# Two first products of layer 1, and the first group's weights, inside the end of an attention

## The chip, the cores and the metric

The kernel runs on one core of a Trainium2 chip. The metric is device time in microseconds (us) of one execution. Before the change three runs took 815.57, 817.38 and 818.75 us; the median is 817.38 us. The traced execution took 815.6 us, of which its trace spans 813.8 us. Times below are counted from the start of that span.

## The reference, cut to what matters

Clustered attention is followed by two feed-forward layers. `x` is the attention's output with the heads side by side (1536 tokens, 512 wide).

```python
scores = np.where(mask, scale * q @ k.T, -1e9)      # B=2, H=8, S=768, D=64; mask: same nearest centroid
attn = softmax(scores); x = attn @ v
h = x @ w_in;   g = np.maximum(0.01 * h, h);  x1 = g @ w_out          # layer 1: 512 -> 2048 -> 512
h = x1 @ w_in2; g = P(h) / (Q(h) + 1e-6);     out = g @ w_out2        # layer 2: P cubic, Q quadratic
```

The weights arrive as 64-bit floats, so each piece of them is rebuilt as a 32-bit number on the core before it is used.

## The kernel before, in words

Every product is made of three matmuls on split numbers (high part times high part, high times low, low times high), so each tensor comes as a pair: `ph`/`pl` for the attention's weights, `xh`/`xl` for `x`, `wih`/`wil` and `woh`/`wol` for the layers' weights, `gh`/`gl` for `g`.

**Attention** works on 96 units of 128 queries (one head, 768 keys). `run` (L674) is a software pipeline written out by hand: iteration i issues, in this order, the row maximum of unit i (DVE), the division of earlier units' `e` (POOL, for the last unit DVE), the transposes `pT` of unit i-4 in two halves, each followed by its cast `ph` on ACT, the `o` matmuls of a group whose last unit this is, exp (ACT), the scores of unit i+1, more `o` matmuls, and `pl = pT - ph` on DVE. The `pT` halves go round three PSUM buffers, so a half waits for the `pl` of the half three before it. Three units make a group; its twelve last `o` matmuls are issued in iterations i+1 to i+3 of its last unit. Then `merge_copy` (ACT, `tmp`), `merge_add` (DVE, `xf`) and, seven iterations later, `finish` (POOL, two or four instructions that write `xh` and `xl`). Each engine runs its instructions in the order in which they are issued here, and what waits holds up all that stands behind it on its engine.

**A piece of weights** (128 x 512) is loaded by SP's queue into a stage (`st`), and rebuilt by ACT (Abs, L787, into `wf`), DVE (a shift, L794, and two merges, L800), ACT (cast to the high part, L807) and POOL (the low part, L810). `Weights.step` issues one such operation of the two oldest pieces in turn. `wsta` is a stage of two buffers, opened in the attention at iteration 84; `wstb`, of two more, lies on memory that the attention has used.

**The layers** run over nine groups of hidden columns. Group 0 of layer 1 has 2 x 128 hidden columns, in a `wi` of two pieces (rebuilt early and kept in a scratch, so only cast and low part are left) and a `wo` of two pieces. A step is (group, token block of 512, 128 hidden columns): twelve `h` matmuls, leaky (ACT, `h<-h`), `gh` (ACT), `gl` (DVE), and three steps later (LAG = 3) twelve `y` matmuls (`back`). Each iteration ends with its share of the next group's rebuilding. `h` has four PSUM buffers, the four `y` have one each; after a block's last step DVE copies them out (`acc`).

In the kernel before, group 0's `wi` is finished in the attention, its `wo` only in part: the pool for it is opened when the attention's memory is free.

Of the kernel before, what the change touches and what calls it, by code (L numbers as in the profile page):

```python
# [17 lines left out]
P = 128  # L18
# [11 lines left out]
def clustered_attention_moe_moe2(  # L30
# [69 lines left out]
    x1 = {}  # L100
# [34 lines left out]
        return a * 2 + u  # L135

    class Attention:
        def __init__(self, actx):
            def pool(nm, bufs, **kw):
                return actx.enter_context(tc.tile_pool(name=nm, bufs=bufs, **kw))  # L140
# [378 lines left out]

        def trans_p(self, u, part):  # L520
            un = self.unit[u]
            pp = self.ring("pT") if u == NU - 1 else self.ptile("pT")
            n = T // 2
            for kt in range(n):
                k0 = (part * n + kt) * P
                nc.tensor.transpose(pp[:, kt * P:(kt + 1) * P], un["e"][:, k0:k0 + P], ident)  # L526
            un["pT", part] = pp[:, 0:n * P].rearrange("p (t n) -> p t n", t=n)
# [146 lines left out]
        def run(self, extra, fill):  # L674
# [10 lines left out]
            for i in range(first, NU + TL + 11):  # L685
# [17 lines left out]
                if live:  # L703
                    self.trans_p(i - TL, 0)
                    self.hi(i - TL, 0)
                    self.trans_p(i - TL, 1)
                    self.hi(i - TL, 1)
                if ok and r == QT - 1:
# [29 lines left out]
                if i == last_prep:  # L738
                    self.pc.close()
                    extra[0]()  # L740
                elif i > last_prep:
                    extra[1](i >= NU + TL)

    class Weights:
        def __init__(self, pools):
# [8 lines left out]
        def add(self, key, src, which, par, wide, store=None):  # L754
# [5 lines left out]

            def alloc():
                pool = self.pools[which, par]
                for x in "hl":
                    t = pool.tile([P, 4, 512], F32R, tag=x, name=f"{which}{x}")
                    hold[x] = t[:, 0:rows // wr].rearrange("p a (b c) -> p (a b) c", c=cols)
# [127 lines left out]

    def queue_group(n):
        for which in ("wi", "wo"):
            if (n, which) in scratch:
                weights.add((which, n), scratch[n, which], which, n % 2, False)
            else:
                weights.add((which, n), weight_source(n, which), which, n % 2, WIDE)

    def queue_scratch(n, whiches=("wi", "wo")):
        for which in whiches:
# [7 lines left out]
    with tc.manual_schedule():  # L910
# [26 lines left out]
        def open_weights(which, par, **kw):  # L937
            wpools[which, par] = wctx.enter_context(
                tc.tile_pool(name=f"{which}{par}", bufs=1, **kw)
            )  # L940

        def open_early():
            while weights.work:
                weights.step()
            weights.wst.clear()
            open_weights("wi", 0, side="right")
            open_stage("wsta", side="right")
            queue_group(0)

        def early_step(late):  # L950
            if late or weights.waits_for(("wi", 0)):
                weights.step(1)

        weights = Weights(wpools)
        with ExitStack() as actx:
            att = Attention(actx)
            att.run((open_early, early_step), (open_start, weights))

        for nm in (("wo", 0), ("wi", 1), ("wo", 1)):
            open_weights(*nm)  # L960
        yp = wctx.enter_context(tc.tile_pool(name="yp", bufs=1))
        x1["c"] = [yp.tile([P, NCT, BLK], F32R, name=nm) for nm in ("xhc", "xlc")]
        accs = yp.tile([P, NCT * NT], F32, name="acc")
        gp_ = wctx.enter_context(tc.tile_pool(name="gp", bufs=3))
        ew = wctx.enter_context(tc.tile_pool(name="ew", bufs=2))
        open_stage("wstb")
        hps = wctx.enter_context(tc.tile_pool(name="hps", bufs=4, space=PSUM))
        yps = wctx.enter_context(tc.tile_pool(name="yps", bufs=1, space=PSUM))
        prep_consts()
        while weights.waits_for(("wi", 0)):  # L970
            weights.step()

        LNC = float(2.0 ** -LN_SHIFT)
        LAG = 3
        steps = [
# [22 lines left out]
        def wide(i):  # L998
            return width(groups[steps[i][0]][0])

        def make_h(i):
            n, j, f = steps[i]
            wih, wil = weights.get(("wi", n))
            w = wide(i)
            hp = hps.tile([P, 512], F32, tag="h", name="h")[:, 0:w]
# [14 lines left out]

        def hi(i):
            d = st[i]
            d["gh"] = gp_.tile([P, 512], F32R, tag="gh", name="gh")[:, 0:wide(i)]
            nc.scalar.copy(d["gh"], d["h"])  # L1024

        def lo(i):
            d = st[i]
            d["gl"] = gp_.tile([P, 512], F32R, tag="gl", name="gl")[:, 0:wide(i)]
            nc.vector.tensor_tensor(d["gl"], d["h"], f32(d["gh"]), op=ALU.subtract)  # L1029

        def leaky(i):
# [91 lines left out]
        def next_x():  # L1123
            j, o, a = later.pop(0)
            t0 = j * 512
            for nm, lo, hi in (("a", 0, 2 * BLK), ("b", 2 * BLK, 3 * BLK), ("c", 3 * BLK, NT)):
# [6 lines left out]
        later = []  # L1133
        for i in range(NS + LAG):
            if i < NS and steps[i][1:] == (0, 0):
                n1 = steps[i][0] + 1
# [2 lines left out]
                if n1 < len(groups):  # L1139
# [13 lines left out]
            if later:  # L1153
                next_x()
            if i >= LAG:
                collect(i - LAG)
# [4 lines left out]
            if i < LAG and weights.waits_for(("wo", 0)):  # L1161
                weights.step(4)
            if i == LAG - 2:
                while weights.waits_for(("wo", 0)):
                    weights.step()


_INS = ['q', 'k', 'v', 'centroids', 'moe_w_in', 'moe_w_out', 'moe2_w_in', 'moe2_w_out', 'moe2_a', 'moe2_b']
# [26 lines left out]
```

## Time and profile before

| what | value |
|---|---|
| median of three runs | 817.38 us |
| traced execution / its span | 815.6 us / 813.8 us |
| PE busy | 789.7 us, 97% of the span |
| DVE, ACT, POOL busy | 660.6, 526.9, 400.4 us |
| last attention unit's exp / first `h` matmul | 263.77 us / 273.99 us |
| first `y` matmul | 285.18 us |

The shares are means over an attention, in which PE, DVE and ACT are all near full, and two layers, in which PE alone is. What the change is worth is read from the stretch from 263 to 300 us, where one passes into the other: there each engine's timeline tells when it was free and what it waited for.

### The profile page before, as it was taken

Reading aid. Unit: us, or ns where it says so; the run is one execution under the profiler, and the core shown is the slowest. Engines: PE = TensorE matmul, PEld = TensorE weight load, DVE = VectorE, ACT = ScalarE, POOL = GpSimd, SP = SyncE. Lnnn points to the kernel's source line nnn. Section 1 sums busy time; section 2 is a strip of 40 time slices with the busy share of each in tenths; the row PEclk is TensorE's granted clock in tenths of the full one; section 3 lists DMA queues with packets and bytes.
Section 4 is the critical chain, followed back from the end, with each engine's and each line's share of the span. In section 5 each row is a group of like instructions: output and inputs, shape, how many; then the busy total and the mean of one; then the engine's idle time right before and its main releaser. Section 6 shows DMA issues by size and latency. Waiting matters only on the chain.

```text
span 813.8 us, 12513 instructions
## 1 busy us (share of the span) xinstructions
PE 789.7 (97%) x4161; PEld 689.7 (85%) x4161; DVE 660.6 (81%) x1198; ACT 526.9 (65%) x1104; POOL 400.4 (49%) x439
## 2 busy tenths in 40 slices
PE   5899999999999999999999999999999999999997
PEld 4889898999888788888888888889988888988995
DVE  6589999989989578877577577768788878888997
ACT  4489888989889454444253345457666667666763
POOL 5568778777675423330031023267555555554442
PEclk9999999999999999999999999999999999999999
DMA  3774654654420233436445444420101010000112
GB/s 103 172 187 101 145 125 102 171 139 91 102 89 1 103 104 122 137 120 217 130 149 186 126 161 127 158 91 27 39 27 39 27 39 27 26 1 1 39 40 78
DMA packets 42256, 78.71 MB, mean 97 GB/s; under 512 B 5328, under 2 KB 25296, under 8 KB 42192
## 3 DMA queue, kind: packets, MB, share of 16 engines
q1 hardware_dynamic: 42192, 77.91, 33.1%
q8 instruction: 33, 0.54, 0.3%
q14 instruction: 31, 0.25, 0.1%
HBM read 49.84 MB, written 9.96 MB: 73 GB/s over the span
## 4 chain that ended last, share of the span: by engine, by line
PE 59%; POOL 13%; DVE 10%; ACT 8%; issue 7%; DMA 0%; POOLq 0%; SPq 0%; DVEq 0%; ACTq 0%
PE h L987 20%; PE y L987 19%; PE o L562 5%; PE s L482 5%; POOL z L1047 5%; PE pT L526 5%; POOL z L1044 3%; DVE pl L545 3%; PE sims L312 2%; DVE nm L491 2%; POOL wol L810 2%; ACT ln L1060 2%; ACT r L1061 2%; POOL wil L810 2%; ACT ph L539 1%
## 5 line engine op out<-in xcount | busy, mean ns | idle before, releaser
L810 POOL TENSOR_TENSOR wil<-wf,wih 128x512 fp32r<-128x512 f32 x32 | 42.8, 1348 | 148.7 <-ACT wih L807 137.1
L518 POOL TENSOR_SCALAR e<-e,sum 128x768 f32<-128x768 f32 x95 | 86.9, 927 | 53.7 <-DVE sum L514 40.0
L545 DVE TENSOR_TENSOR pl<-pT,ph 128x384 fp32r<-128x384 f32 x192 | 97.3, 546 | 17.1 <-ACT ph L539 16.5
L1024 ACT CAST gh<-h 128x384 fp32r<-128x384 f32 (+1 forms) x112 | 58.9, 526 | 79.9 <-DVE h L1068 52.1
L1029 DVE TENSOR_TENSOR gl<-h,gh 128x384 fp32r<-128x384 f32 (+1 forms) x112 | 68.2, 609 | 40.4 <-ACT gh L1024 40.2
L491 DVE TENSOR_REDUCE nm<-s 128x1 f32<-128x768 f32 x96 | 91.0, 948 | 6.9 <-PE s L482 6.4
L987 PE MATMUL h<-xha,wil 128*128 128x512 f32 (+1 forms) x256 | 93.5, 365 | 0.0
L987 PE MATMUL h<-xha,wih 128*128 128x512 f32 (+1 forms) x256 | 93.3, 364 | 0.0
L987 PE MATMUL h<-xla,wih 128*128 128x512 f32 (+1 forms) x256 | 93.3, 364 | 0.0
L539 ACT CAST ph<-pT 128x384 fp32r<-128x384 f32 x192 | 82.3, 481 | 15.4 <-PE pT L526 14.0
L502 ACT ACTIVATE e<-s,nm 128x768 f32<-128x768 f32 x96 | 87.4, 910 | 7.2 <-DVE nm L491 3.6
L526 PE MATMUL pT<-ident,e 128*128 128x128 f32 x576 | 81.6, 276 | 3.0 <-DVE pl L545 2.8
L800 DVE SCALAR_TENSOR_TENSOR wf<-st,wf 128x512 int32<-128x512 int32 x124 | 83.6, 727 | 0.0
L1044 POOL TENSOR_SCALAR z<-y,abv 128x384 f32<-128x384 f32 x64 | 43.1, 673 | 73.1 <-ACT y L1040 73.1
L987 PE MATMUL y<-woh,gl 128*128 128x512 f32 x192 | 76.4, 398 | 0.7 <-DVE gl L1029 0.3
L987 PE MATMUL y<-woh,gh 128*128 128x512 f32 x192 | 76.2, 397 | 0.8 <-ACT gh L1024 0.6
L987 PE MATMUL y<-wol,gh 128*128 128x512 f32 x192 | 75.2, 392 | 0.0
L526 PEld LDWEIGHTS pT<-ident,e 128*128 128x128 f32 x576 | 68.0, 143 | 8.4 <-DVE pl L545 3.5
L987 PE MATMUL y<-gh,wol 128*128 128x512 f32 x192 | 75.0, 390 | 0.0
L987 PE MATMUL y<-gl,woh 128*128 128x512 f32 x192 | 74.8, 390 | 0.0
L987 PE MATMUL y<-gh,woh 128*128 128x512 f32 x192 | 74.8, 390 | 0.0
L810 POOL TENSOR_TENSOR wol<-wf,woh 128x512 fp32r<-128x512 f32 x32 | 41.7, 1312 | 66.4 <-ACT woh L807 52.3
(123 smaller groups left out, 2050.1 us busy)
## 6 DMA issues: line engine op xcount, KB each, us to landing
st<-in_moe_w_out_dram SPq DMA_DIRECT2D x32, 512.0 KB, 4.7
st<-in_moe_w_in_dram SPq DMA_DIRECT2D x30, 512.0 KB, 4.7
a<-hl SPq DMA_DIRECT2D x56, 192.0 KB, 3.6
b<-hl SPq DMA_DIRECT2D x28, 192.0 KB, 5.7
wf<-scratch_wi SPq DMA_DIRECT2D x14, 256.0 KB, 2.5
qraw<-in_q_dram SPq DMA_DIRECT2D x16, 192.0 KB, 2.9
kraw<-in_k_dram SPq DMA_DIRECT2D x16, 192.0 KB, 3.4
vraw<-in_v_dram SPq DMA_DIRECT2D x8, 384.0 KB, 5.8
```

The source lines that it names most:

```text
L491: nc.vector.reduce_max(un["nm"], un["s"][:, 0:S], axis=AX.X, negate=True)
L502: nc.scalar.activation(un["e"], un["s"][:, 0:S], AF.Exp, bias=un["nm"], accum_out=un["recip"])
L518: eng.tensor_scalar(un["e"], un["e"], un["recip"], 1.0, op0=ALU.mult, op1=ALU.mult)
L526: nc.tensor.transpose(pp[:, kt * P:(kt + 1) * P], un["e"][:, k0:k0 + P], ident)
L539: nc.scalar.copy(un["hi", part], un["pT", part])
L545: nc.vector.tensor_tensor(self.group[gi]["pl"][:, part * n:(part + 1) * n, i * P:(i + 1) * P], un["pT", part], f32(un["hi", part]), op=ALU ...
L800: nc.vector.scalar_tensor_tensor(wi, hold["st", i][:, :, :, 1 - w], sc, wi, op0=op, op1=ALU.bitwise_or)
L810: nc.gpsimd.tensor_tensor(hold["l"][:, i:i + wr, :], hold["wf", i], f32(hold["h"][:, i:i + wr, :]), op=ALU.subtract,)
L987: nc.tensor.matmul(o, lhsT=l, rhs=r, start=(first and idx == 0), stop=(last and idx == n - 1),)
L1024: nc.scalar.copy(d["gh"], d["h"])
L1029: nc.vector.tensor_tensor(d["gl"], d["h"], f32(d["gh"]), op=ALU.subtract)
L1044: nc.gpsimd.tensor_scalar(d["z"], d["y"], abv[:, 1:2], abv[:, 0:1], op0=ALU.mult, op1=ALU.add)
```

## The change

1. `wi` and `wo` of group 0 get a pool of their own (`w0`, "near") on the side of memory that the attention's preparation has left at iteration 84, and the pool for `gh`/`gl` moves there too. So all of group 0's weights can be rebuilt before the attention ends.
2. `early_h` makes step 0's `h` in iteration 96, and step 1's in iteration 97, between the two halves of the transposes of unit 92 and of unit 93. They lie in one of the two score buffers; the last unit's transposes, which used those, go round the three `pT` buffers instead.
3. `early_step` at the end of iterations 97 to 103 does three rebuilding operations, and in 97 and 98 the leaky step, `gh` and `gl` of steps 0 and 1.
4. The layer then begins with `back(0)` and `back(1)`, followed by the `h` of steps 2 to 5. `prep_consts` moves to iteration 3. `xhc`/`xlc` take the near pool's place later on. The pools of the layer are opened in another order, so `wstb` lies a little lower.

```diff
         def trans_p(self, u, part):
             un = self.unit[u]
-            pp = self.ring("pT") if u == NU - 1 else self.ptile("pT")
+            pp = self.ptile("pT")
...
                     self.trans_p(i - TL, 0)
                     self.hi(i - TL, 0)
+                    if i >= NU:
+                        extra[2](i - NU)
                     self.trans_p(i - TL, 1)
...
                 elif i > last_prep:
-                    extra[1](i >= NU + TL)
+                    extra[1](max(0, i - NU + 1))
...
     def queue_group(n):
         for which in ("wi", "wo"):
+            par = n % 2 if n else "near"
...
-            open_weights("wi", 0, side="right")
+            late["w0"] = wctx.enter_context(tc.tile_pool(name="w0", bufs=1, side="right"))
+            for which in ("wi", "wo"):
+                wpools[which, "near"] = late["w0"]
             open_stage("wsta", side="right")
+            late["gp"] = wctx.enter_context(tc.tile_pool(name="gp", bufs=3, side="right"))
             queue_group(0)
 
-        def early_step(late):
-            if late or weights.waits_for(("wi", 0)):
+        def early_step(n):
+            if n == 0 and weights.waits_for(("wi", 0)):
                 weights.step(1)
-
+            if 1 < n < 9:
+                weights.step(3)
+                if n - 2 < EARLY:
+                    leaky(n - 2)
+
+        def early_h(i):
+            if i < EARLY:
+                if i == 0:
+                    while weights.waits_for(("wi", 0)):
+                        weights.step()
+                    late["h"] = att.ring("h")
+                into_h(i, late["h"][:, i * 512:i * 512 + wide(i)])
+
+        late = {}
+        EARLY = 2
...
-            if i < NS:
+            if EARLY <= i < NS:
                 make_h(i)
-            if i >= LAG:
-                back(i - LAG)
-            if 0 <= i - 1 < NS:
+            done = i if i < EARLY else i - LAG if i - LAG >= EARLY else -1
+            if done >= 0:
+                back(done)
+            if i == LAG:
+                prep_consts()
+            if EARLY <= i - 1 < NS:
                 start(i - 1)
```

How this moves instructions shows best on DVE and in SP's queue. First DVE, from the `pl` of unit 92 to the first `gl` of the layer proper; before:

```order
L545 TENSOR_TENSOR pl<-pT,ph 128x3x128 x2
L583 TENSOR_TENSOR xf<-o,tmp 64x384
L545 TENSOR_TENSOR pl<-pT,ph 128x3x128 x6
L583 TENSOR_TENSOR xf<-o,tmp 64x384
L794 TENSOR_SCALAR wf<-wf 128x512
L583 TENSOR_TENSOR xf<-o,tmp 64x384
L794 TENSOR_SCALAR wf<-wf 128x512
L800 SCALAR_TENSOR_TENSOR wf<-st,wf 128x512 x4
L94 TENSOR_SCALAR nav<-av 128x4
L95 TENSOR_SCALAR nbv<-bv 128x2
L96 TENSOR_TENSOR abv<-bv,nbv 128x2
L1029 TENSOR_TENSOR gl<-h,gh 128x512
```

And after the change, from the `pl` of unit 93 to the first copy of `y`:

```order
L545 TENSOR_TENSOR pl<-pT,ph 128x3x128 x2
L801 TENSOR_SCALAR wf<-wf 128x512 x2
L1039 TENSOR_TENSOR gl<-h,gh 128x512
L545 TENSOR_TENSOR pl<-pT,ph 128x3x128 x2
L807 SCALAR_TENSOR_TENSOR wf<-st,wf 128x512 x3
L1039 TENSOR_TENSOR gl<-h,gh 128x512
L545 TENSOR_TENSOR pl<-pT,ph 128x3x128 x2
L583 TENSOR_TENSOR xf<-o,tmp 64x384
L807 SCALAR_TENSOR_TENSOR wf<-st,wf 128x512
L583 TENSOR_TENSOR xf<-o,tmp 64x384
L801 TENSOR_SCALAR wf<-wf 128x512 x2
L1119 COPY acc<-y_3972 128x512
```

The six `pl` of units 93 to 95 stood in a row and now have two shifts and a `gl` between units 93 and 94, and three merges and a `gl` between units 94 and 95. The last two shifts above, of group 1's `wi`, stand ahead of the copies of `y`.

Second, the loads that SP issues from group 0's `wo` (the first row) on, with what each waits for; before:

```order
L775 DMA st<-in_moe_w_out_dram 128x1024 x2
L775 DMA st<-in_moe_w_in_dram 128x2x512 [waits DVE_49,Pool_49]
L775 DMA st<-in_moe_w_in_dram 128x2x512
L775 DMA st<-in_moe_w_out_dram 128x1024 [waits DMAHW3_49,DVE_49]
L775 DMA st<-in_moe_w_out_dram 128x1024 [waits DMAHW4_49,DVE_49]
```

And after:

```order
L782 DMA st<-in_moe_w_out_dram 128x1024 x2
L782 DMA st<-in_moe_w_in_dram 128x2x512 [waits DMAHW3_49,DVE_49,Activation_49]
L782 DMA st<-in_moe_w_in_dram 128x2x512 [waits DVE_49,Pool_49]
L782 DMA st<-in_moe_w_out_dram 128x1024 [waits DMAHW4_49]
L782 DMA st<-in_moe_w_out_dram 128x1024
```

The first piece of group 1's `wi` now goes to `wsta`, which the rebuilding of `wo` leaves free; the second goes to `wstb`, and the wait on POOL moves to it. The two pieces of `wo` stand behind it in both.

## Rows read from the trace of the kernel before

**Rows 1.** Windows: stretch, us, busy us of PE PEld DVE ACT POOL, clock, DMA, GB/s

```profile
24.00:28.00 4.00, 4.00 (x19) 3.71 (x17) 1.92 (x2) 0.99 (x2) 0.73 (x1) 1.00 0.16 42
...
300.00:813.00 513.00, 508.55 (x2385) 436.39 (x2383) 406.91 (x700) 288.08 (x538) 200.65 (x205) 1.00 0.26 88
```

**Rows 2.** Timeline of PE: start, us, what, xcount [idle before <-what ended it]

```profile
22.89 0.42 PE L370 MATMUL po<-identr,oh 128*96 128x128 f32 x2 [5.10 <-DVE oh L358]
...
263.39 0.49 PE L526 MATMUL pT<-ident,e 128*128 128x128 f32 x3
264.15 0.55 PE L526 MATMUL pT<-ident,e 128*128 128x128 f32 x3 [0.28 <-DVE pl L545]
...
265.25 0.49 PE L526 MATMUL pT<-ident,e 128*128 128x128 f32 x3
267.21 0.55 PE L526 MATMUL pT<-ident,e 128*128 128x128 f32 x3 [1.47 <-DVE pl L545]
268.14 0.45 PE L562 MATMUL o<-ph,vs 128*128 128x384 f32 x1 [0.38 <-DVE xf L583]
...
270.32 0.82 PE L526 MATMUL pT<-ident,e 128*128 128x128 f32 x6
270.89 0.42 PE L562 MATMUL o<-ph,vs 128*128 128x384 f32 x1
...
273.99 0.39 PE L987 MATMUL h<-xha,wih 128*128 128x512 f32 x1
...
285.18 0.40 PE L987 MATMUL y<-gh,woh 128*128 128x512 f32 x1
```

**Rows 3.** Timeline of DVE, the attention's end and the layer's start

```profile
266.61 1.01 DVE L545 TENSOR_TENSOR pl<-pT,ph 128x384 fp32r<-128x384 f32 x2
...
275.62 3.62 DVE L800 SCALAR_TENSOR_TENSOR wf<-st,wf 128x512 int32<-128x512 int32 x4
...
284.66 0.69 DVE L1029 TENSOR_TENSOR gl<-h,gh 128x512 fp32r<-128x512 f32 x1 [5.07 <-ACT gh L1024]
285.27 0.75 DVE L794 TENSOR_SCALAR wf<-wf 128x512 int32<-128x512 int32 x2
285.93 1.29 DVE L800 SCALAR_TENSOR_TENSOR wf<-st,wf 128x512 int32<-128x512 int32 x2
...
293.76 2.47 DVE L1109 COPY acc<-y 128x512 f32<-128x512 f32 x4
```

**Rows 4.** Timeline of ACT, the same stretch

```profile
270.84 0.86 ACT L539 CAST ph<-pT 128x384 fp32r<-128x384 f32 x2 [0.49 <-PE pT L526]
...
281.63 0.66 ACT L787 ACTIVATE wf<-st 128x512 f32<-128x512 f32 x1 [2.28 <-DMA st<-in_moe_w_in_dram]
...
289.54 0.60 ACT L807 CAST wih<-wf 128x512 fp32r<-128x512 f32 x1
290.05 0.58 ACT L1033 ACTIVATE h<-h 128x512 f32<-128x512 f32 x1
290.66 0.59 ACT L1024 CAST gh<-h 128x512 fp32r<-128x512 f32 x1
```

**Rows 5.** Timeline of POOL, the same stretch

```profile
258.25 0.40 POOL L601 TENSOR_SCALAR xha<-xf 128x256 fp32r<-128x256 f32 x1
...
259.82 0.46 POOL L602 TENSOR_TENSOR xlb<-xf,xhb 128x128 fp32r<-128x128 f32 x1
...
264.68 0.51 POOL L601 TENSOR_SCALAR xhb<-xf 128x384 fp32r<-128x384 f32 x1
265.28 1.00 POOL L602 TENSOR_TENSOR xlb<-xf,xhb 128x384 fp32r<-128x384 f32 x1
...
279.43 1.32 POOL L810 TENSOR_TENSOR wol<-wf,woh 128x512 fp32r<-128x512 f32 x1 [1.94 <-ACT woh L807]
```

**Rows 6.** SP's queue, timeline of the layer's first loads

```profile
277.51 0.89 SPq L775 DMA_DIRECT2D st<-in_moe_w_in_dram  x2
```

**Rows 7.** SP's queue, 270 to 280 us: what it waited for, us, times, longest

```profile
SPq L775 <- POOL xlb L602: 2.2, 1, 2.2
```

More of the change, by code (lines that the diff above doesn't have):

```diff
@@ L137, in clustered_attention_moe_moe2, with __init__ @@
     class Attention:
-        def __init__(self, actx):
+        def __init__(self, actx, pctx):
             def pool(nm, bufs, **kw):
-                return actx.enter_context(tc.tile_pool(name=nm, bufs=bufs, **kw))
+                return (pctx if kw else actx).enter_context(tc.tile_pool(name=nm, bufs=bufs, **kw))
             self.sm = pool("sm", 2)
@@ L762, in alloc @@
                 pool = self.pools[which, par]
+                if par == "near":
+                    t = pool.tile([P, 2, rows * cols], F32R, tag=which, name=f"{which}near")
+                    for n, x in enumerate("hl"):
+                        hold[x] = t[:, n].rearrange("p (a c) -> p a c", c=cols)
+                    return
                 for x in "hl":
@@ L895, in queue_group @@
         for which in ("wi", "wo"):
+            par = n % 2 if n else "near"
             if (n, which) in scratch:
-                weights.add((which, n), scratch[n, which], which, n % 2, False)
+                weights.add((which, n), scratch[n, which], which, par, False)
             else:
-                weights.add((which, n), weight_source(n, which), which, n % 2, WIDE)
+                weights.add((which, n), weight_source(n, which), which, par, WIDE)
     def queue_scratch(n, whiches=("wi", "wo")):
@@ L945, in open_early @@
             weights.wst.clear()
-            open_weights("wi", 0, side="right")
+            late["w0"] = wctx.enter_context(tc.tile_pool(name="w0", bufs=1, side="right"))
+            for which in ("wi", "wo"):
+                wpools[which, "near"] = late["w0"]
             open_stage("wsta", side="right")
+            late["gp"] = wctx.enter_context(tc.tile_pool(name="gp", bufs=3, side="right"))
             queue_group(0)
-        def early_step(late):
-            if late or weights.waits_for(("wi", 0)):
+        def early_step(n):
+            if n == 0 and weights.waits_for(("wi", 0)):
                 weights.step(1)
-        weights = Weights(wpools)
[L955 to L971, printed above, removed]
+            if 1 < n < 9:
[11 more added lines that the diff above has]
+        EARLY = 2
+        weights = Weights(wpools)
+        pctx = ExitStack()
         LNC = float(2.0 ** -LN_SHIFT)
@@ L1001, in make_h, with into_h @@
         def make_h(i):
+            into_h(i, hps.tile([P, 512], F32, tag="h", name="h")[:, 0:wide(i)])
+        def into_h(i, hp):
             n, j, f = steps[i]
@@ L1004, in make_h @@
             w = wide(i)
-            hp = hps.tile([P, 512], F32, tag="h", name="h")[:, 0:w]
             if rational(i):
@@ L1022, in hi @@
             d = st[i]
-            d["gh"] = gp_.tile([P, 512], F32R, tag="gh", name="gh")[:, 0:wide(i)]
+            d["gh"] = late["gp"].tile([P, 512], F32R, tag="gh", name="gh")[:, 0:wide(i)]
             nc.scalar.copy(d["gh"], d["h"])
@@ L1027, in lo @@
             d = st[i]
-            d["gl"] = gp_.tile([P, 512], F32R, tag="gl", name="gl")[:, 0:wide(i)]
+            d["gl"] = late["gp"].tile([P, 512], F32R, tag="gl", name="gl")[:, 0:wide(i)]
             nc.vector.tensor_tensor(d["gl"], d["h"], f32(d["gh"]), op=ALU.subtract)
@@ L1125, in next_x @@
             t0 = j * 512
+            if "c" not in x1:
+                x1["c"] = [
+                    late["w0"].tile([P, NCT, BLK], F32R, tag=t, name=nm)
+                    for t, nm in (("wi", "xhc"), ("wo", "xlc"))
+                ]
             for nm, lo, hi in (("a", 0, 2 * BLK), ("b", 2 * BLK, 3 * BLK), ("c", 3 * BLK, NT)):
@@ L1133, in clustered_attention_moe_moe2 @@
         later = []
+        with ExitStack() as actx:
+            att = Attention(actx, pctx)
+            att.run((open_early, early_step, early_h), (open_start, weights))
+        while weights.waits_for(("wo", 0)):
+            weights.step()
+        pctx.close()
+        for nm in (("wi", 0), ("wo", 0), ("wi", 1), ("wo", 1)):
+            open_weights(*nm)
+        yp = wctx.enter_context(tc.tile_pool(name="yp", bufs=1))
+        accs = yp.tile([P, NCT * NT], F32, name="acc")
+        ew = wctx.enter_context(tc.tile_pool(name="ew", bufs=2))
+        open_stage("wstb")
+        yps = wctx.enter_context(tc.tile_pool(name="yps", bufs=1, space=PSUM))
+        hps = wctx.enter_context(tc.tile_pool(name="hps", bufs=4, space=PSUM))
         for i in range(NS + LAG):
@@ L1154, in clustered_attention_moe_moe2 @@
                 next_x()
-            if i >= LAG:
-                collect(i - LAG)
+            if done >= 0:
+                collect(done)
             if 0 <= i - 1 < NS and rational(i - 1):
@@ L1160, in clustered_attention_moe_moe2 @@
             weights.step(max(0, due - (total - weights.pending())))
[L1161 to L1165, printed above, removed]
 _INS = ['q', 'k', 'v', 'centroids', 'moe_w_in', 'moe_w_out', 'moe2_w_in', 'moe2_w_out', 'moe2_a', 'moe2_b']
```

## The prediction, made before the change was timed

> **What bounds the kernel now.** I read the windows first. From 300 us to the end PE is busy 508.55 of 513.00 us [rows 1], so a delay of PE before 300 us is not made good later, and time saved for PE there is kept. Then PE's timeline where attention passes into the layer [rows 2]. The reader is to see three gaps. A half transpose (three matmuls) keeps PE 0.29 us: six take 0.57, from 270.32 to 270.89. So PE is free at 263.68 and goes on at 264.15 (0.47 us), is free at 265.54 and goes on at 267.21 (1.67), is free at 267.50 and goes on at 268.14 (0.64). The first two end on a `pl` of DVE, the third on DVE's `xf`. Together 2.8 us; gaps under 0.15 us I leave out on both sides. From 270.32 on PE streams, and the layer's first `h` starts at 273.99 without a gap. There 48 matmuls take 11.19 us to 285.18, so 0.233 each, 2.80 for one `h` product. Last I read DVE, ACT and POOL over the same stretch, to see how soon they can serve what is moved [rows 3 to 5].
>
> **The change part by part.** I lay the new order on the engines, each instruction at the spacing of its rows, starting from 263.39, up to which nothing differs.
>
> The two `h` products, 24 matmuls, 5.60 us, are the same work in another place. At 5.60 us the gaps above are filled twice over, so 2.8 us of idle time go. This is the whole of what can be gained here.
>
> What is late next: DVE. PE runs the first product from 263.68 to 266.48, the second half of unit 92 and four `o` (0.79 us) to 267.56, the first half of unit 93 and the second product to 270.65, then the rest of unit 93 to 271.7, unit 94 with its `o` to 273.1, and the first half of unit 95 to 273.4. The second half of unit 95 needs the `pT` buffer that the first `pl` of unit 94 frees. That `pl` stands behind new instructions. On ACT, `ph` of unit 93 (0.43 spacing from the pair of 0.86 [rows 4]) starts at 271.2, Abs of `wo` at 271.6, leaky at 272.2, `gh` at 272.8 to 273.4, and only then `ph` of unit 94, to 273.8. On DVE, `pl` of unit 93 starts at 271.7, two shifts (0.375 each) follow, `gl` waits for `gh` and runs 273.4 to 274.0 (0.61 spacing, row 0.69), and the first `pl` of unit 94 ends at 274.6. PE waits 1.3 us.
>
> Then DVE does the other `pl` of unit 94 (0.47), three merges and the second `gl` before `pl` of unit 95. Two merges took 1.29 us at 285.93, when POOL was idle, and four took 3.62 at 275.62, when it was at work [rows 3]. POOL has nothing here between 266.3, when it ends the `xlb` begun at 265.28 [rows 5], and the first `wo` at 277.7, so I take 0.645 each: 275.0 to 276.9, `gl` to 277.5, `pl` of unit 95 ends at 278.1. PE has done the `o` before and one of the last twelve by 276.0, and waits 2.1 us for it. The last twelve end at 280.0.
>
> So attention's end loses 1.3 + 2.1 = 3.4 us and wins 2.8: 0.6 us net. Before, PE had two products more to do at 273.99, which is 279.6 with them; now it is at 280.0. By bounds: no new wait gives -2.8; merges at 0.905 give 0.26 x 3 = 0.8 more, +1.4.
>
> The other operations that move to ACT and POOL here cost PE nothing: `wo`'s casts and low parts are done by 281.6 (a low part 1.32 us [rows 5]), and `back(1)` asks for the second at 282.8.
>
> The second cost is in the layer. SP's loads of group 1 waited for POOL's last `xlb` before, 2.2 us [rows 7], and went out at 277.51 [rows 6]; the last `xlb` is that of `finish` for the last group. Now the second piece of `wi` waits for that, and the last `xlb` comes later: POOL does the two low parts of `wo` first, to 281.6, then six copies. Four of these took 2.0 us (258.25 to 259.82 + 0.46) and two 1.6 (264.68 to 266.28) [rows 5], so 285.2. The load lands 4.1 us after issue (277.51 to 281.63, where ACT had waited for it [rows 4]): 289.4.
>
> Behind it stand, on ACT, Abs of this piece (0.66), and only after it the first piece's cast, an Abs, the second cast, an Abs, and then leaky of step 2. On DVE the shift of this piece stands ahead of four copies of `y` (2.47), four merges, and the `gl` of step 2 [rows 3]. So: Abs ends 290.1, shift 290.5, copies 293.0, third merge 295.0, the four on ACT 2.2 us (a cast 0.51 to the next, an Abs about 0.57, its 0.66 less the same overlap) to 297.2, leaky 0.61 and `gh` 0.59 to 298.4, `gl` to 299.2. PE comes to the `y` of step 2 at 280.0 + 24 `y` and 48 `h` matmuls, at 0.233 all of them = 296.8 (296.7 at `y`'s slightly closer spacing). Its first matmul needs `gh`, its second `gl`: it waits 1.8 and then 0.5 us, 2.3 in all. Before, the loads were out at 277.51 while PE had 11.19 us of `h` before it, and this chain was hidden. Bounds: 0, if the chain is 2.3 us shorter than I make it; at the other end 3.9, with POOL's copies at 1.3 times these rows (0.26 x 3.6 = 1.1) and 0.5 us more of merges. I take the middle, because all its terms but the landing are in rows.
>
> After that ACT and DVE catch up: `gl` of step 3 is due at 304.8 and done by about 302, of step 4 at 310 and done by 306. No further wait.
>
> `prep_consts`, three instructions, lies in DVE's chain in both. The near pool's later use, and the exchange of the banks of `h` and `y`, I put at nothing: the first is needed only when layer 1 ends, the second moves no instruction.
>
> Sum: -2.8 + 3.4 + 2.3 = +2.9 us. On the profiled execution's 815.6 us that is 818.5. The median, 817.38, lies 1.8 us above that execution; the change to it gives 820.3 us, or 0.35% more. A difference under 0.5%, 4.1 us, can't be told from no change by a measurement of this kernel. The same way of laying it out, for the order before, gives 2.9 us of idle and the first `y` at 285.1 against 285.18 in the trace.
>
> **The rivals.** *Only the first cost.* The late load is hidden by the four `h` products: +0.6, 818.0 us. For it: 11.2 us of `h` stand between; against it: the chain from the load's issue to `gl` is 14 us and PE has 11.5 from that issue.
>
> *Faster.* Neither DVE nor the load delays PE, the gaps are filled: -2.8, 814.6 us. For it: PE now waits 1.67 us at once in a place that gets 2.8 us of work. Against it: the six `pl` of units 93 to 95 stood in a row and are now cut by two `gl`, two shifts and three merges, 4 us of DVE. It decides if `pl` of unit 95 ends before 276.
>
> *Clearly slower.* The second cost is dearer: POOL's copies, the load and the merges get in each other's way. With 0.905 for each merge (0.8 in attention, 1.0 in the layer), copies 1.3 times as long (1.1) and 0.6 more until landing: +3.5, so +6.4 and 823.8 us. It passes 0.5% from a `gl` of step 2 at 300.4, 1.2 us later than I put it.
>
> *The clock.* PE waited 5.10 us until 22.89, and from 24 to 28 us the granted clock was 1.00, 2.4 GHz, with PE busy throughout [rows 1, 2]. So waits of 2.1 us need not cost clock. Were PE at 1.2 GHz for one `h` product after either wait, 2.8 us would be 5.6: +2.9 + 2.8 = +5.7, 823.1 us. [...]
>
> **How the numbers follow.** The forecast has 0.58, only the first cost 0.17, faster 0.07, clearly slower 0.15, the clock 0.03. Faster by over 0.5% (under 813.3): nobody's case reaches it, 0.02 for what I have not seen. Slower by over 0.5% (above 821.5): 0.11 of the 0.15, the clock's 0.03, and 0.06 of the forecast's own spread: 0.20. Within: 0.78. The range reaches from 816.0, under the first rival by the runs' own spread, to 823.0, into the clearly slower case; the forecast's own is 818.5 to 821.7.
>
> **What would show it.** Right: `h` matmuls on PE between the transposes of units 92 and 93; a wait of PE of about 1.3 us before a half transpose and of about 2 us between the first and second of the last twelve `o`, both on DVE's `pl`; the first `y` 6 us after 273.99; a load in SP's queue that waits for `xlb` until about 285; and a wait of PE on `gh` and `gl` at the third block of `y`. Wrong: a stream on PE without these waits (faster), or without the last (only the first cost), or any window with a clock below 1.00.

## The result and the profile after

The changed kernel takes 821.5 us (median of five executions, 821.18 to 821.94); the kernel before, run beside it, 817.38 us. The ratio is 1.0058 (95% interval 1.0041 to 1.0075): slower, by 4.1 us where 2.9 were forecast. The traced execution took 821.5 us, its span is 819.7 us, 5.9 more than before's 813.8. PE's starts tell where they lie. Layer 1 has 48 blocks of twelve `y` matmuls; behind the 45th, the `h` of layer 2 begin to stand between them.

| stretch of PE | before | after | more |
|---|---|---|---|
| to the first half transpose of unit 92 | 263.39 | 263.71 | 0.32 |
| from there to the ninth `y` block of layer 1 (328.98, 332.10 us) | 65.59 | 68.39 | 2.80 |
| from there over 36 blocks to the 45th (526.90, 532.26 us) | 197.92 | 200.16 | 2.24 |
| from there to the unbroken run of `y` that ends layer 2 (799.55, 805.47 us) | 272.65 | 273.21 | 0.56 |

What is left is 14.2 us in both. The second row is the passage that the forecast laid out. The third it did not have at all: there no instruction moved and PE waits for nothing. First the passage, on PE's timeline of the changed kernel (start, duration, engine, line, operation; in brackets the idle time and who ended it):

```profile
263.71 0.49 PE L526 MATMUL pT<-ident,e 128*128 128x128 f32 x3
263.95 0.48 PE L995 MATMUL h<-xha,winear 128*128 128x512 f32 x1
...
268.11 0.48 PE L995 MATMUL h<-xha,winear 128*128 128x512 f32 x1
...
273.37 0.49 PE L526 MATMUL pT<-ident,e 128*128 128x128 f32 x3
274.93 0.55 PE L526 MATMUL pT<-ident,e 128*128 128x128 f32 x3 [1.07 <-DVE pl L545]
...
276.07 0.44 PE L562 MATMUL o<-ph,vs 128*128 128x384 f32 x1
278.26 0.69 PE L562 MATMUL o<-pl,vs 128*128 128x384 f32 x1 [1.74 <-DVE pl L545]
...
279.06 0.52 PE L562 MATMUL o<-pl,vs 128*128 128x384 f32 x1
279.38 0.52 PE L562 MATMUL o<-ph,vs 128*128 128x384 f32 x1
...
281.81 0.39 PE L995 MATMUL y<-gh,wonear 128*128 128x512 f32 x1
...
298.48 0.40 PE L995 MATMUL y<-gh,wonear 128*128 128x512 f32 x1
299.08 0.50 PE L995 MATMUL y<-gl,wonear 128*128 128x512 f32 x1 [0.21 <-DVE gl L1039]
```

They answer to [rows 2]: the three gaps there (2.8 us) are gone, the two products stand in them, and two waits on `pl` have come, in the places foretold. The `o` matmuls after the second wait start 0.32 us apart, where they are 0.17 to 0.18 apart otherwise. The windows of the same stretch (window, its length, busy time and count of each engine; then the granted clock of PE) say why:

```profile
277.00:278.00 1.00, 0.00 (x0) 0.00 (x0) 1.00 (x3) 0.62 (x1) 0.13 (x1) 1.00 0.00 0
278.00:278.50 0.50, 0.24 (x1) 0.24 (x2) 0.50 (x2) 0.00 (x0) 0.50 (x1) 0.73 0.65 86
...
279.00:280.00 1.00, 1.00 (x4) 1.00 (x4) 0.95 (x2) 0.00 (x0) 0.14 (x1) 0.50 0.79 293
...
281.50:282.00 0.50, 0.50 (x4) 0.50 (x3) 0.00 (x0) 0.00 (x0) 0.50 (x2) 0.86 0.00 0
```

PE stood still from 277 to 278 us, and from 278.2 to 281.6 its clock is 0.50 (1.2 GHz). Below, "the drop" is such a fall of the granted clock. DVE's timeline, which answers to [rows 3], has the queue that the forecast laid out:

```profile
272.75 0.76 DVE L801 TENSOR_SCALAR wf<-wf 128x512 int32<-128x512 int32 x2 [0.17 <-issue]
273.72 0.69 DVE L1039 TENSOR_TENSOR gl<-h,gh 128x512 fp32r<-128x512 f32 x1 [0.20 <-ACT gh L1034]
274.32 1.01 DVE L545 TENSOR_TENSOR pl<-pT,ph 128x384 fp32r<-128x384 f32 x2
275.25 1.89 DVE L807 SCALAR_TENSOR_TENSOR wf<-st,wf 128x512 int32<-128x512 int32 x3
277.06 0.68 DVE L1039 TENSOR_TENSOR gl<-h,gh 128x512 fp32r<-128x512 f32 x1
277.66 1.01 DVE L545 TENSOR_TENSOR pl<-pT,ph 128x384 fp32r<-128x384 f32 x2
```

SP's queue has the late load too; it is now the second piece of `wi` that stands behind POOL's last `xlb` (waits of SP's queue: total, times, longest), as [rows 7] had the first:

```profile
SPq L782 <- POOL xlb L602: 2.5, 1, 2.5
```

Now the stretch where nothing waits. One block of twelve `y` and one of twelve `h` on PE, before:

```profile
328.98 0.39 PE L987 MATMUL y<-gh,woh 128*128 128x512 f32 x1
...
331.71 0.39 PE L987 MATMUL h<-xha,wih 128*128 128x512 f32 x1
...
334.51 0.39 PE L987 MATMUL y<-gh,woh 128*128 128x512 f32 x1
```

and after:

```profile
332.10 0.40 PE L995 MATMUL y<-gh,woh 128*128 128x512 f32 x1
...
334.91 0.40 PE L995 MATMUL h<-xha,wih 128*128 128x512 f32 x1
...
337.66 0.40 PE L995 MATMUL y<-gh,woh 128*128 128x512 f32 x1
```

Twelve `y` took 2.73 us and take 2.81; twelve `h` took 2.80 and take 2.75. The clock is 1.00 in both. Over the 36 blocks the `y` take 2.69 us more and the `h` 0.45 us less, which is the 2.24. What differs is where the operands lie: `gh`/`gl` were at byte 154048 of each partition and are at 188384, which is 32 past a multiple of 64; `wi` of the even groups was at 212960 (high part) and 221152 (low part), also 32 past one, and is at 68032 and 76224, which are multiples. The near pool, with group 0's `wi` and `wo` and later `xhc`/`xlc`, lies at 212960 and 221152 after the change.

### The profile page after: what moved, and what is told of

Its sections match the earlier page's. It is cut to its first block, busy times and chain, and to the rows that moved or that the text cites. A ratio compares the mean times of both kernels' runs of the same rounds, so it can differ in the third digit from the quotient of the medians.

```text
span 819.7 us, 12509 instructions
## 1 busy us (share of the span) xinstructions
PE 795.1 (97%) x4161; PEld 692.1 (84%) x4161; DVE 661.0 (81%) x1198; ACT 526.7 (64%) x1104; POOL 400.7 (49%) x439
## 4 chain that ended last, share of the span: by engine, by line
PE 56%; POOL 14%; DVE 12%; ACT 9%; issue 7%; DMA 1%; POOLq 0%; SPq 0%; DVEq 0%; ACTq 0%
PE y L995 19%; PE h L995 19%; POOL z L1057 5%; PE s L482 5%; PE o L562 5%; PE pT L526 5%; POOL z L1054 3%; DVE pl L545 3%; PE sims L312 2%; DVE nm L491 2%; POOL wol L817 2%; ACT ln L1070 2%; ACT r L1071 2%; POOL wil L817 2%; ACT ph L539 1%
## 5 line engine op out<-in xcount | busy, mean ns | idle before, releaser
L817 POOL TENSOR_TENSOR wil<-wf,wih 128x512 fp32r<-128x512 f32 x30 | 40.3, 1356 | 151.1 <-ACT wih L814 144.5
L995 PE MATMUL h<-xha,wih 128*128 128x384 f32 (+1 forms) x240 | 87.4, 364 | 0.0
L995 PE MATMUL h<-xha,wil 128*128 128x384 f32 (+1 forms) x240 | 87.0, 363 | 0.0
L995 PE MATMUL h<-xla,wih 128*128 128x384 f32 (+1 forms) x240 | 86.6, 361 | 0.0
L807 DVE SCALAR_TENSOR_TENSOR wf<-st,wf 128x512 int32<-128x512 int32 x124 | 81.4, 710 | 0.0
L562 PE MATMUL o<-ph,vs 128*128 128x384 f32 x192 | 69.3, 361 | 0.0
L1121 DVE TENSOR_TENSOR acc<-y,acc 128x512 f32<-128x512 f32 x84 | 55.7, 687 | 16.5 <-PE y L995 16.2
L817 POOL TENSOR_TENSOR wol<-wf,woh 128x512 fp32r<-128x512 f32 x30 | 39.1, 1313 | 60.6 <-ACT woh L814 49.9
L1057 POOL TENSOR_TENSOR z<-z,y 128x384 f32<-128x384 f32 x64 | 65.4, 1022 | 5.3
```

The source lines that it names most:

```text
L562: nc.tensor.matmul(gr["o"], lhsT=self.pair[p]["vs"][:, h * T + tile_of(kt), :], rhs=gr["pl" if j else "ph"][:, kt, :], start=n == 0, stop= ...
L807: nc.vector.scalar_tensor_tensor(wi, hold["st", i][:, :, :, 1 - w], sc, wi, op0=op, op1=ALU.bitwise_or)
L817: nc.gpsimd.tensor_tensor(hold["l"][:, i:i + wr, :], hold["wf", i], f32(hold["h"][:, i:i + wr, :]), op=ALU.subtract,)
L995: nc.tensor.matmul(o, lhsT=l, rhs=r, start=(first and idx == 0), stop=(last and idx == n - 1),)
L1057: nc.gpsimd.tensor_tensor(d["z"], d["z"], d["y"], op=ALU.mult)
```

## The experiments

The passage is told by the time from unit 92's first half transpose to the ninth `y` block (65.59 before, 68.39 after), the layer by the 36 blocks behind it (197.92, 200.16).

**e1: the kernel before, once more**, unedited.

> The kernel before, unchanged, for a second trace of it. Its runs lie 3.2 us apart (815.57 to 818.75), those of the changed kernel 0.8. Theory A: before has executions with and without something that costs 1.6 to 3 us, such as a stretch of 3.4 us at 1.2 GHz in the gaps at the attention's end; then this trace, if it comes from an execution of 817 us or more, shows a mean clock under 1.000 or a first y later than 285.2 us. Theory B: the spread lies ahead of 263 us or in the layers, with the clock at 1.00 throughout; then the stretch from 263 to 302 us is as in the first trace.

817.52 us, ratio to before 1.0007 (0.9992 to 1.0023). The 36 blocks take 197.92 again, but the passage 67.07, 1.48 more than in the trace that the forecast was made from. On PE stands the gap of [rows 2]:

```profile
268.17 0.55 PE L526 MATMUL pT<-ident,e 128*128 128x128 f32 x3 [1.48 <-DVE pl L545]
```

and its windows have

```profile
267.00:268.00 1.00, 0.00 (x0) 0.00 (x0) 1.00 (x2) 0.79 (x2) 0.23 (x1) 1.00 0.00 0
268.00:269.00 1.00, 0.55 (x3) 0.31 (x3) 1.00 (x4) 0.24 (x1) 0.00 (x0) 0.99 0.03 8
269.00:270.00 1.00, 0.91 (x3) 0.91 (x4) 0.97 (x3) 0.24 (x1) 0.00 (x0) 0.50 0.00 0
...
271.00:272.00 1.00, 1.00 (x6) 1.00 (x5) 0.07 (x1) 0.48 (x1) 0.00 (x0) 0.50 0.00 0
```

So the kernel before has executions with a drop of the clock after that gap and others without; the one that was traced first had none. Of the 29 executions of before that ran beside e5 to e8, 11 have a mean clock of 0.999 or 1.000 (median 816.24 us) and 11 one of 0.995 to 0.998 (median 818.27). All five of the changed kernel have 0.997 or 0.998. The other 7 of before lie at 0.989 to 0.993 and are the quickest (median 815.09), so a lower mean doesn't mean a longer time. In the three traces with such a mean (e4, e9, e10) the clock is 0.50 from 21 or 22 us to about 32 us, ahead of the attention, and yet unit 8 starts at 54.33 to 55.32 us where it starts at 56.84 in before's first trace. Why is not shown, and the starts of these traces can't be held against those of the others.

**e2: before, `gh`/`gl` where the change puts them.**

```diff
+            late["gp"] = wctx.enter_context(tc.tile_pool(name="gp", bufs=3, side="right"))
...
-        gp_ = wctx.enter_context(tc.tile_pool(name="gp", bufs=3))
```

> The kernel before with the pool of gh and gl where the changed kernel has it (from 154048 to 188384 in a partition's bytes), nothing else. After 302 us the changed kernel loses 2.6 us more in layer 1, in which a y matmul starts 0.234 us after the one before it where it was 0.227. Theory A, the place of gh and gl: y spacing 0.234 here too, and the stretch of layer 1 from the y block at 302 to its last y takes 217 us instead of 214; the kernel is 3 us slower, 0.35%. Theory B, the exchange of the PSUM banks of h and y, or the place of the weights: 0.227 and 214, no change in time.

821.55 us, ratio 1.0051 (1.0033 to 1.0069), the 36 blocks 201.11 us. One moved pool, with no instruction moved, costs as much as the whole change.

**e3: the changed kernel, `h` in banks 0 to 3 and `y` in 4 to 7 as before.**

```diff
+        hps = wctx.enter_context(tc.tile_pool(name="hps", bufs=4, space=PSUM))
         yps = wctx.enter_context(tc.tile_pool(name="yps", bufs=1, space=PSUM))
-        hps = wctx.enter_context(tc.tile_pool(name="hps", bufs=4, space=PSUM))
```

> The changed kernel with h in PSUM banks 0 to 3 and y in 4 to 7, as before the change. Theory A, the place of gh and gl: y spacing stays 0.234, layer 1's stretch stays 216.7; the first y waits about 1 us for the attention's last xf, so the time is the same to +1 us. Theory B, the banks: spacing 0.227, 2.6 us faster than the changed kernel in that stretch, some 0.2 to 0.3% in all.

821.71 us, ratio to before 1.0059 (1.0037 to 1.0080); the 36 blocks 200.16, the same to the hundredth. The exchange of the banks costs nothing, as forecast; undone, it lengthens the passage by 0.82 us (69.21), since the first `y` then waits.

**e4: the changed kernel, both pieces of group 1's `wi` in the stage that is free early**, so that neither load waits for POOL's last `xlb`.

```diff
-                slot = min(self.wst, key=lambda w: w["used"] - w["room"])
+                slot = self.wst[0] if key == ("wi", 1) else min(self.wst, key=lambda w: w["used"] - w["room"])
```

> The changed kernel with both pieces of group 1's wi in the stage wsta, so that neither load waits for POOL's last xlb. Theory A (the second term of the prediction): the second load goes out at about 279.5 instead of 285.5, PE no longer waits on gh and gl at the third block of y, and the blocks after it come 0.8 us earlier (what the trace of the changed kernel shows of this wait; 2.3 us were forecast). Theory B: the wait moves to a load of wo, and nothing is gained. The stretch at 1.2 GHz near 278 to 282 us stays in both.

821.18 us, ratio 1.0048 (1.0027 to 1.0068): no difference to the changed kernel that can be told. In the trace the wait at the third block of `y` is gone:

```profile
275.46 0.44 PE L562 MATMUL o<-pl,vs 128*128 128x384 f32 x1 [1.74 <-DVE pl L545]
275.74 0.34 PE L562 MATMUL o<-ph,vs 128*128 128x384 f32 x1
275.92 0.34 PE L562 MATMUL o<-pl,vs 128*128 128x384 f32 x1
...
277.48 0.39 PE L995 MATMUL y<-gh,wonear 128*128 128x512 f32 x1
...
294.14 0.39 PE L995 MATMUL y<-gh,wonear 128*128 128x512 f32 x1
294.38 0.40 PE L995 MATMUL y<-gl,wonear 128*128 128x512 f32 x1
```

Against what was expected, that execution had no drop of the clock in the passage, though both waits on `pl` stand in it with the same 1.07 and 1.74 us: the `o` behind the second start 0.18 us apart. Its passage is 66.37, 2.02 less than after. The first `y` comes 16.57 us after unit 92 began (at 260.91), where after has 18.10: 1.53 for the drop, near e1's 1.48. The 0.49 that is left is the load.

**e5 and e6: is it the side of the memory or the multiple of 64?** e5 is before with 32 bytes ahead of the pool of `gh`/`gl` (and 32 behind it), e6 the changed kernel with 32 bytes ahead of it (the last two lines):

```diff
+        wctx.enter_context(tc.tile_pool(name="pad", bufs=1)).tile([P, 8], F32, name="pad")
         gp_ = wctx.enter_context(tc.tile_pool(name="gp", bufs=3))
+        wctx.enter_context(tc.tile_pool(name="pad2", bufs=1)).tile([P, 8], F32, name="pad2")
...
+            wctx.enter_context(tc.tile_pool(name="pad", bufs=1, side="right")).tile([P, 8], F32, name="pad")
             late["gp"] = wctx.enter_context(tc.tile_pool(name="gp", bufs=3, side="right"))
```

> The kernel before with one edit: the pool of gh and gl begins 32 bytes higher, at 154080 instead of 154048 (a second piece of 32 bytes behind it keeps all that follows at multiples of 64). Theory A: what costs is that gh and gl don't begin at a multiple of 64 bytes; at 154048 they do, at 188384 (run e2) they lie 32 past one. Then this run has the y matmuls of layer 1 at .234 us instead of .227, the stretch of 36 blocks of y that ends layer 1 takes 201.1 us as in e2 instead of 197.9, and the ratio to before is 1.004 to 1.005. Theory B: what costs is the side of the memory (the right end, beside stages and weights); then 32 bytes change nothing: 197.9 us and a ratio of 1.000.

> The changed kernel with one edit: 32 bytes between the stage and the pool of gh and gl, so that this pool begins at 188352, a multiple of 64, still at the right end of the memory. Theory A (a multiple of 64 bytes): the last 36 blocks of y in layer 1 take about 197.0 us (200.16 less the 3.2 of e2), below the 197.9 of before, since the weights of even groups also lie at multiples of 64 now; time about 817.5, ratio to before 1.000, which leaves the +2 us of attention's end made good by the weights. Theory B (the side of the memory): 200.2 us, 821.5, ratio 1.005.

e5: 821.18 us, ratio 1.0065 (1.0044 to 1.0086), the 36 blocks 201.11 as in e2. On its PE, to be held against the block of before and after above:

```profile
331.50 0.40 PE L989 MATMUL y<-gh,woh 128*128 128x512 f32 x1
...
334.31 0.40 PE L989 MATMUL h<-xha,wih 128*128 128x512 f32 x1
```

e6: 817.2 us, ratio 1.0011 (0.9999 to 1.0023), the 36 blocks 195.84:

```profile
333.01 0.39 PE L996 MATMUL y<-gh,woh 128*128 128x512 f32 x1
...
335.73 0.39 PE L996 MATMUL h<-xha,wih 128*128 128x512 f32 x1
```

Twelve `y` take 2.81 us in e5, 2.72 in e6. Theory A holds on both sides; B, the side of the memory, has fallen. Thirty-two bytes make the changed kernel as fast as the one before, and in e6 the layer is quicker than before (195.84 against 197.92) because its `wi` lies well too; I had 197.0 for it, 1.2 too much.

**e7 and e8: all operands of matmuls at multiples of 64**, in the kernel before and in the changed one.

```diff
+    ctx.enter_context(tc.tile_pool(name="padr", bufs=1, side="right")).tile([P, 8], F32, name="padr")
...
+            pool("pad", 1).tile([P, 8], F32, name="padl")
             self.tr = pool("tr", 2)
```

> The kernel before with two edits: 32 bytes at the right end of the memory and 32 bytes behind attention's small tiles, so that all operands of matmuls (a, b, vs, e, ph, pl in attention, wi of even groups in the layers) begin at multiples of 64; before, these lay 32 past one. Theory A: each matmul that streams such an operand starts .007 us sooner after the one before; the h of even groups (.2322 a matmul now, .2267 in odd groups, 744 matmuls) gives 3 to 5 us, of which 1.1 in the last 36 blocks of layer 1 (197.9 to 196.8); attention gives between 0 (if ACT and DVE hold it) and 9 us (some 1350 matmuls by .007). Time 805 to 814, ratio .985 to .996. Theory B: nothing moves to another side, ratio 1.000.

> The changed kernel with the two edits of e7, which put all its operands at multiples of 64 (gh and gl too, and xhc and xlc in the near pool). Theory A: what is left of the change's loss is attention's end alone (the waits on pl and the clock after them): 0 to 2 us above run e7, and the same 36 blocks within .3 us of e7's. Theory B: as the changed kernel, 821.5, ratio 1.005.

e7: 814.69 us, ratio 0.9974 (0.9959 to 0.9990), above the range expected. e8: 816.86 us, ratio 1.0003 (0.9992 to 1.0014). Both have 195.84 us for the 36 blocks, 0.2267 a matmul for `h` and `y` alike (864 of them): 2.08 less than before, where 1.1 was expected. Layer 2 gave nothing: 273.07 and 273.11 us in the fourth row of the table, above before's 272.65 although all operands lie well. Attention gave nothing either: from unit 8 to unit 92 it takes 206.56 us before, 206.91 in e7 and 206.70 in e8, and its `o`, 384 columns wide, start 0.17 to 0.18 us apart at either place. e8 is 2.2 us above e7, just over the 0 to 2 expected. In the traces, which both have the drop, the passage is 67.95 and 66.83, so 1.1 of it is the passage. The rest isn't taken apart; of the twelve executions, three of e7 have a mean clock of 0.999 or 1.000 and none of e8, so how often the drop comes may have a part in it.

**e9: e8 with PE kept at work in the two waits** by matmuls that nobody reads. This part of the edit makes them; it is called at two places, cut here.

```diff
...
+                for n in range((4, 8)[i - 3]):
+                    nc.tensor.matmul(
+                        late["fill"][:, (i - 3) * 512:(i - 2) * 512], lhsT=wih[:, n % NCT, 0:P],
+                        rhs=x1["a"][0][:, n % NCT, 0:512], start=True, stop=True,
+                    )
```

> Run e8 (the changed kernel, all operands at multiples of 64) with matmuls that nobody reads put into the two waits of PE at attention's end: 4 of 128x512 ahead of the second half transpose of unit 95, 8 ahead of the second of the last twelve o. They take .9 and 1.8 us, a little less than PE stood there in e8 (1.3 and 2.0 between the neighbours' ends and starts), so pl comes no earlier and PE is held up no longer. Theory A (the clock falls because PE pauses there): no stretch at 0.50 near 279 us; from the first h product to the first y it takes 15.3 us in place of e8's 16.87, and the time is 815.3, .998 of e8's. Theory C (the drop comes at this place whatever PE does in the waits): 16.9 us, 816.9. Either way the wait at the third block of y grows by what the first y gains, up to 1.5 us, if group 1's late load sets it: then the clock's price is partly hidden behind the load, and the time stays at 816 to 817.

817.81 us, ratio 1.0004 (0.9989 to 1.0020), as e8. On its PE:

```profile
270.98 1.18 PE L986 MATMUL fill<-xha,winear 128*128 128x512 f32 x4
...
273.72 2.00 PE L986 MATMUL fill<-xha,winear 128*128 128x512 f32 x8
...
295.87 0.51 PE L1009 MATMUL y<-gh,wonear 128*128 128x512 f32 x1 [1.75 <-ACT gh L1048]
296.59 0.50 PE L1009 MATMUL y<-gl,wonear 128*128 128x512 f32 x1 [0.22 <-DVE gl L1053]
```

and the windows behind the third block of `y`:

```profile
294.00:296.00 2.00, 0.25 (x2) 0.13 (x1) 0.62 (x2) 1.97 (x5) 1.67 (x2) 1.00 0.91 295
296.00:298.00 2.00, 1.78 (x6) 1.25 (x7) 2.00 (x5) 0.89 (x2) 0.00 (x0) 0.90 0.45 184
298.00:300.00 2.00, 2.00 (x6) 1.53 (x5) 2.00 (x4) 0.36 (x1) 0.00 (x0) 0.50 0.04 8
```

With the waits filled the first `y` comes at once, at 277.64, and no drop comes there. PE then meets the late load with nothing spent before it: it waits 1.75 and 0.22 us for `gh` and `gl`, and the drop follows that wait. Its passage, 69.61, is even 1.66 longer than e8's. The place of the drop is as Theory A has it, but one trace doesn't show it: e4's has no drop there either, with the waits unfilled. The time doesn't fall, by the second half of what was expected.

**e10 and e11: e8 with `wo` rebuilt earlier**, one operation in each iteration up to 95, the two leaky steps an iteration later, and the load of e4. e11 moves one product instead of two.

```diff
+            if n == 0 and not weights.waits_for(("wi", 0)):
+                weights.step(1)
...
-                if n - 2 < EARLY:
-                    leaky(n - 2)
+            if 3 <= n < 3 + EARLY:
+                leaky(n - 3)
```

> Run e8 with the rebuilding out of the way of pl: one operation of wo's pieces in each iteration from where wi is done on (iterations 88 to 95) in place of three in each of 97 to 103, the two leaky steps one iteration later (98 and 99), and group 1's wi both in the stage that is free first, so that its load doesn't wait for POOL's last xlb. Nothing else differs: the two h products stand where the change puts them. Theory A (DVE's queue holds pl up, the waits bring the clock down, the late load holds gh and gl up): both waits on pl shrink from 1.06 and 1.74 to under .4 and .7 us, none at the third block of y, no stretch at 0.50 there in most executions; the layout by rows gives 4.3 us less idle than the changed kernel, 1.9 less than before; time about 812.5, ratio to before .995, 2 us under e7. Rival: the operations brought forward delay the attention (DVE and ACT are near full in it) by as much as the end wins: unit 92 starts 1 to 3 us later and the time is 815 or more.

> As e10, but with one h product moved into the attention in place of two (its leaky step at iteration 98). Theory A: the first product fills the gap of 1.67 us, the second fills gaps of .6 us only and delays units 93 to 95; so one is as good as two: 812.5, within 1 us of e10. Rival (the second product is needed to cover waits on xf and pl): 1 to 1.5 us slower than e10.

e10: 816.7 us, ratio 0.9997 (0.9983 to 1.0011); e11: 816.82 us, 1.0006 (0.9992 to 1.0019). The passage is as expected, 62.98 us from unit 92 on, with 0.36 us left of the waits on `pl`. e11 has 63.03 there, so one product is as good as two, as expected. But the attention comes later, the rival, and by more than its 1 to 3 us: from unit 85 to unit 92 it takes 21.06 us in e10 where it takes 15.22 in e8 (20.76 in e11). Of the 5.84 more, 3.64 lie between units 85 and 87, and 2.20 behind, with three waits of 0.23, 0.43 and 0.70 us on PE. The first part is one wait, on ACT, where `wo`'s first Abs stands ahead of a `ph`:

```profile
247.95 0.68 ACT L796 ACTIVATE wf<-st 128x512 f32<-128x512 f32 x1 [1.40 <-POOL winear L819]
```

and on PE

```profile
249.63 0.55 PE L528 MATMUL pT<-ident,e 128*128 128x128 f32 x3 [1.86 <-DVE pl L547]
```

with the drop right behind it:

```profile
250.00:252.00 2.00, 1.87 (x8) 1.55 (x7) 2.00 (x5) 1.73 (x5) 0.00 (x0) 0.67 0.00 0
252.00:254.00 2.00, 2.00 (x11) 1.91 (x9) 1.44 (x4) 0.92 (x4) 0.40 (x1) 0.50 0.03 8
```

**e12: one product early, `wo` rebuilt behind `pl`, the layer in its old order**, meant to beat both kernels.

```diff
-            if 1 < n < 9:
-                weights.step(3)
+            if n >= 3:
+                weights.step(1)
...
-            done = i if i < EARLY else i - LAG if i - LAG >= EARLY else -1
+            done = i - LAG
...
+            if begin == 0:
+                due = total * min(max(i - EARLY + 1, 0), 4) // 4
```

> A version meant to beat both kernels: all operands at multiples of 64 as in e7 and e8; one h product of layer 1 in the gap of 1.67 us between the halves of unit 92; wo rebuilt by one operation in each iteration from 99 on, so that nothing new stands ahead of the pl of units 93 and 94 and only one operation or two ahead of that of unit 95; the first leaky step in iteration 100; then the layer in its old order (two more h products before the first y, a lag of three steps), so that wo and the first gl have those products as cover, and group 1's rebuilding begins with the second step. Theory A (what cost was the DVE work ahead of pl, the late load behind y, and the operands' place): no wait of PE above 1 us between 263 and 300 us, the layout by rows leaves 1.6 us idle there against 2.95 in e7; no stretch at 0.50 at attention's end in most executions; 1.3 to 2.5 us under e7's 814.7, so 812 to 813.5, ratio to before .994 to .996. Rival: the drop of the clock or a new wait comes at another place of the passage, and the time is that of e7 or more, 814.7 to 817.

815.48 us, ratio 0.9984 (0.9964 to 1.0003): no better than e7. No drop and one wait of 0.57 us up to 283 us, but then, as the rival has it,

```profile
297.40 0.47 PE L997 MATMUL y<-gh,wonear 128*128 128x512 f32 x1 [2.43 <-DVE acc L1121]
```

because DVE had come to the copies of `y` late, behind group 1's rebuilding, itself late by its load, which had waited 4.3 us for POOL's last `xlb` and for which ACT's Abs waited until 286.95. On DVE's timeline:

```profile
287.64 0.43 DVE L803 TENSOR_SCALAR wf<-wf 128x512 int32<-128x512 int32 x1 [4.25 <-ACT wf L796]
...
296.58 2.47 DVE L1121 COPY acc<-y 128x512 f32<-128x512 f32 x4
```

By the medians the fastest kernel found is thus e7, the one before with 64 bytes of padding, though its interval and e12's overlap.

## Why the prediction was right or wrong

- **The gaps filled, -2.8:** right. All three are gone.
- **New waits on `pl`, 1.3 + 2.1:** right. By the same reckoning PE stands 1.27 us (from 273.37 + 0.29 to 274.93) and 2.02 us (from 276.07 + 0.17 to 278.26).
- **The late load, 2.3:** the mechanism was right, the size wrong: 0.37 us in the changed kernel (299.08 less 298.48, less the 0.23 of a matmul). The chain was laid out well: `gl` of step 2, forecast to end at 299.2, ends at 299.0. But PE comes to that block at 298.5 in place of 296.8: the forecast had it there without the drop, which made it late by 1.5 us and so hid the load. e9, without a drop ahead of it, has 2.4 us there by the same count.
- **The clock, at 0.03:** the step that failed is "waits of 2.1 us need not cost clock", drawn from one wait ahead of the attention. A window with a clock below 1.00, which the forecast named as a sign of being wrong, came. e1 shows the drop behind before's own gap of 1.48 us, e9 and e10 behind waits of 1.75 and 1.86. Its price is 1.5 us (e1, and after against e4), not 2.8 or more. The Trainium skill, "TensorE: Matmul & The Clock Gate", section "HAM oscillation", has a wait of PE between matmuls halve the clock, and speaks of waits longer than these. Here e1, e9 and e10 have the drop behind waits of 1.48 to 1.86 us, and before's first trace and e4's have none behind 1.47 and 1.74.
- **The base:** "the change to it gives 820.3" carried 1.8 us from the traced execution to the median as if they were noise. The traced execution lacked the drop, and executions of before with the mean clock of a drop are 2.0 us longer in the median than those without (818.27, 816.24), so most of the 1.8 is probably the drop. Against an execution of before that has it, the clock cost nothing new.
- **"The near pool's later use, and the exchange of the banks ... I put at nothing":** the banks are nothing (e3). The place of `gh`/`gl` isn't in the sum at all, though the first point of the change names it; e2, e5 and e6 show that it is the largest term. In the 36 blocks it costs 4.32 us (200.16 less e6's 195.84), of which `wi`'s new place gives back 2.08 (197.92 less 195.84). Ahead of them all places together cost 0.44 (68.39 less e8's 67.95); that isn't `gh`/`gl` alone, since e6 has 68.37 there, and the near weights lie 32 past a multiple too. The 0.56 of layer 2 isn't explained by the places: e8 has 0.46 of it with all operands at multiples. Its cause stays open.

The sum as measured, against the traced execution: -2.8 + 3.3 + 0.4 for the passage, 1.5 for the clock, 2.7 for the places, 0.6 in layer 2, 0.3 by which unit 92 came later: 6.0, of 5.9. Against e1, which has the drop as the changed kernel has it, the rows of the table give 1.32 + 2.24 + 0.56 = 4.1 us, the difference of the medians. The forecast had 2.9 for the passage, where 0.9 was due, and nothing for the places and layer 2, where 3.3 came. So 820.3 came near 821.5 by luck, by errors that cancelled in part; what came is just over 0.5%, to which the forecast gave 0.20.

## What to carry to other kernels

A diff that moves a pool moves addresses: compare the byte address of every matmul operand before and after, and pad to 64. What is shown here is for 128x512 matmuls of 32-bit operands. Before a cost is read from one trace, look whether the repeated times fall into two groups, and which of them the trace is from. Work that is moved into a gap of the bound engine must not bring its followers ahead of what that engine waits for next; the time it takes from one wait is otherwise given back at the next (e9, e10, e12).

## What the runs showed of the hardware

"Streamed" is the operand named first behind the arrow on a matmul's line of the profile (`rhs` in the code of e9), "stationary" the second (`lhsT`). A 128x512 matmul whose streamed operand began 32 bytes past a multiple of 64 followed the one before after 0.2330 to 0.2337 us (means of twelve; after, e2, e5) in place of 0.2267 (e6 to e8); with such a stationary operand (`wi` of even groups, before) it was 0.2329. That is 3%, about 1/32, and a row of a streamed operand is 32 pieces of 64 bytes, so one piece more would fit; no run here shows the mechanism. Against so simple a reading, the `h` of the changed kernel, whose operands all lie at multiples, take 0.2298 between its `y`, and 0.2267 in e6, where only `gh`/`gl` moved. Why 384 columns didn't suffer is open.

The clock fell to 0.50 for about 3.4 us behind waits of 1.48 to 1.86 us; the fall began at the wait's end (after) to 1.7 us later (e9). It didn't come behind each such wait: before's first trace (a 1.47 us wait) and e4's (1.74) have none in the passage. What decides that between executions of one kernel stays open.
